# A gated mix of a Fourier layer and 32-head attention on one core: named PSUM banks and a freed value bank in the 52 short sections

## The chip, the cores and the metric

The kernel runs on one core of a Trainium2 chip. The metric is the device time of one execution in microseconds (us); lower is better. A core has a matrix engine (TensorE, PE in the profile; its weight loads are PEld), a vector engine (VectorE, DVE), an activation engine (ScalarE, ACT), GpSimd (POOL) and SyncE (SP), which here issues most of the transfers. Each engine runs its own instructions in their order and waits on semaphores for the others. PE writes its results to PSUM, eight banks of 128 partitions x 512 fp32 numbers; here ACT and DVE read them out.

## The reference

```python
x = A_x                                            # 1 x 2048 x 512
g = sigmoid((x * gate_w).sum(-1, keepdims=True))
a = Ws_re @ (x @ Wd_re.T) - Ws_im @ (x @ Wd_im.T)  # Fourier mixing: 512 wide, then 2048 long
q, k, v = split(B_x @ wqkv)                        # B_x is x; 32 heads of 16
p = softmax(q @ k.T * 16 ** -0.5)                  # per head, 2048 x 2048
b = (p @ v, heads put side by side) @ wo
out = g * a + (1 - g) * b
```

All in fp32. The inputs of the products are split into a high and a low part, and three products stand for one.

## The kernel before, in words

After the projections of q, k and v the kernel is one long stream. Attention is done per pair of heads `p` (16 pairs) and per half of the queries. The work on it comes in three kinds:

- **a**, a product for a maximum (`a_tile`, L291): 128 queries x 512 keys into a bank; DVE then takes the row maximum (L293).
- **s**, a score (`scores`, L795): 128 keys x 512 queries into a bank; ACT then writes its exponential to a tile `pt` in SBUF (L796). Four scores fill one `pt`, called a unit `u`.
- **values** (`pv`, L843): for one unit, four products of `pt` with `vt`, added up in the bank `acc`. `vt` has a column of ones beside each head's values, so that the sum of the exponentials comes out as a further row.

a and s have 64 rows or fewer, half of PE's array, and run beside a **d** on the other half: a product of the other layer (L469), whose 128 rows are cut into two halves. The first half of a d chain is done in one segment, the second half in the next. So PE's work goes in *slots*: two products side by side, mostly a d and one of a and s, sometimes (a "double") two of a and s without a d.

`segment` walks a pattern, written out by hand, one word for each slot. A small letter is the a or s beside the d; a second, capital letter makes the slot a double, whose second product is from the other half's stream; `|` is the four value products of one unit. A digit behind a letter names the bank. Each segment has eight a and eight s on average and two units of values. There are three kinds of segments:

| pattern | segments | slots in them | d chains | order and place of values |
|---|---|---|---|---|
| `THIN` | 13 pairs | 14 and 14 | `real`, 12 products | before the last 4 slots, and at the end |
| `FULL` | 96 pairs | 16 and 16 | `dft`, 48 products over three pairs | both at the end |
| `NINE` | 13 pairs | 12 and 13 | `proj`, 9 products | before the last 3 or 4 slots, and at the end |

Of the eight banks one is `d`, and seven are numbered. In `FULL` every a and s names its bank, 0 to 6: bank 6 is that of `acc`, and it can take an a and a score, because at a FULL segment's end the values are closed (`close`): ACT copies `acc` to an SBUF tile `part` (L822; the first one goes to `oe`, L816), POOL adds that to a running total `oe` (L823), and the next segment's values begin a fresh sum. In `THIN` and `NINE` the letters have no digits. There a `Ring` gives the bank used longest ago: scores among 0, 1, 2, maxima among 3, 4, 5. Bank 6 keeps `acc` alone, and it is copied only when a pair of heads is done with one half of the queries (every 16 units, eight segments) and once at the end of `THIN`.

A d chain ends in one ACT copy of bank `d`: `y` in `THIN` (L485), `few` in `NINE` (L665, followed by a POOL add, L666). The next chain's first d waits for it. Between the two halves of a chain, the second half's first d is made to wait (`add_manual_dep`) for the reader of one product that stood behind the first half's last d: the exponential of the *last* such s, or the maximum of the first such a where there is no s.

Of the kernel before, what the change touches and what calls it, by code (L numbers as in the profile page):

```python
# [20 lines left out]
NP = H // 2  # L21
KT = D // P
NT = S // P
# [8 lines left out]
def mix_kernel(ctx: ExitStack, tc: tile.TileContext, xa_t, xa, wqkv, w_hid, w_seq, wo, gate_w, out):  # L32
# [227 lines left out]
    vt = main.tile([P, NT, NP, 33], F32, name="vt")  # L260
# [24 lines left out]
    def a_tile(i, h, ps=None, bank=None):  # L285
        p, j = divmod(i, 64)
        qt, kb = divmod(j, 4)
        if ps is None:
            ps = psA.tile([P, 512], F32, "a", bank)
        r = slice(64 * h, 64 * h + (64 if p else 48))  # L290
        nc.tensor.matmul(ps, qs[p % 2][r, qt * P:(qt + 1) * P], ks[p % 2][r, kb * 512:(kb + 1) * 512],  # L291
                         start=True, stop=True)
        user = nc.vector.tensor_reduce(mx[p % 2][:, h, qt, kb:kb + 1], ps, AX.X, ALU.max)  # L293
        hf = j // 32
        a_left[p, hf] = a_left.get((p, hf), 64) - 1
        if not a_left[p, hf]:
            deferred.extend((partial(m_parts, p, hf), partial(m_rows, p, hf)))
        return user
# [483 lines left out]
    def scores(u, qb, h, bank=(psS, "s"), number=None):  # L782
        p, r = divmod(u, 32)
        hf, kt = divmod(r, 16)
        q0 = hf * 1024 + qb * 512
        if u >= UNITS - 16:

            blk, kt = divmod(kt, 8)
            q0, kt = 1024 + blk * 512, 2 * kt + qb
        if u not in pts:  # L790
            pts[u] = work.tile([P, 4, 512], F32, name="pt", bufs=4)
        pool, name = bank
        ps = pool.tile([P, 512], F32, name=name) if number is None else pool.tile([P, 512], F32, name, number)
        rr = slice(64 * h, 64 * h + (64 if p else 50))
        nc.tensor.matmul(ps, ks[p % 2][rr, kt * P:(kt + 1) * P], qs[p % 2][rr, q0:q0 + 512], start=True, stop=True)  # L795
        return nc.scalar.activation(pts[u][:, 2 * qb + h], ps, AF.Exp, bias=0.0, scale=DH ** -0.5)  # L796

    def pv_last(u):
        blk, k2 = divmod(u - UNITS + 16, 8)
        pt = pts.pop(u)  # L800
        for j in range(4):
            x, h = divmod(j, 2)
            nc.tensor.matmul(acc[32 * j:32 * j + 17], vt[:, 2 * k2 + x, NP - 1, 16 * h:16 * h + 17], pt[:, j],  # L803
                             start=k2 == 0, stop=k2 == 7)
        if blk == 0 and k2 == 7:
            last_pairs.append(LastPair(0, [(psS, "s"), (psA, "a")]))
            last_pairs[0].copy(1)
# [3 lines left out]
    def evacuate(p, hf, done):  # L811

        nonlocal total
        if total is None:
            total = work.tile([P, 512], F32, name="oe", bufs=2)
            nc.scalar.copy(total, acc)  # L816
        else:
            if not part:
                two = work.tile([P, 2, 512], F32, name="part", tag="w15")
                part.extend(two[:, i] for i in range(2))  # L820
            part.reverse()
            nc.scalar.copy(part[0], acc)  # L822
            nc.gpsimd.tensor_tensor(total, total, part[0], ALU.add)  # L823
        if done:
            for qb in range(2):
                nc.sync.dma_start(o_d[hf][p, :, qb * 512:(qb + 1) * 512], total[64 * qb:64 * qb + 64])
            total = None

    def pv(u, close=False):
        nonlocal acc  # L830
        if u >= UNITS - 16:
            return pv_last(u)
        p, r = divmod(u, 32)
        hf, kt = divmod(r, 16)
        pt = pts.pop(u)
        begin, done, width = acc is None or kt == 0, kt == NT - 1, 17
        if acc is None:
            acc = psO.tile([P, 512], F32, "acc")
            width = 32
        v = vt[:, kt].rearrange("p n d -> p (n d)")[:, 33 * p:]  # L840
        for j in range(4):
            h = j % 2
            i = nc.tensor.matmul(acc[32 * j:32 * j + width], v[:, 16 * h:16 * h + width], pt[:, j],  # L843
                                 start=begin, stop=done or close)
        if done or close:
            evacuate(p, hf, done)
            if close:
                acc = None
        return i
# [35 lines left out]
    for hf in range(2):  # L885
        for ct in range(4):
            n = 3 if hf and ct == 3 else 4
# [31 lines left out]

    FULL = "a5 s4 a2 s0 a3 s6 a5 s4 s1 s0 s2 a6 a3 a4 s5 a1 | |"  # L920
    START = "sA s aS - - a s - - a s - - a", "s a s a s a s a s a s a +s +a"
    THIN = "s a s a s a s a s a | s a aS sA |", "aS a s s a s a s a s | s a a sA |"
    NINE = "a s a s a s a s a | sS sA aA |", "aS s a s a s s a aS | s a sA sA |"

    def stream(h):

        return (
            iter([(u, qb, h) for u in range(UNITS) for qb in range(2)]),
            iter([(i, h) for i in range(lead, NP * 64)]),
        )  # L930

    thin = 1 + 4 * (NT - 3)
    streams = [stream(h) for h in range(2)]

    users, valued, exponentials = [], 0, []

    def score(kind, h, number=None):
        x = next(streams[h][kind == "a"], None)
        if x:
            users.append((kind, a_tile(*x, bank=number) if kind == "a" else scores(*x, number=number)))  # L940
            if kind == "s":
                exponentials.append(users[-1][1])

    def values(close=False):
        nonlocal valued
        i = pv(valued, close)
        valued += 1
        return i

    def segment(pattern, half, ds, stop):  # L950


        nonlocal users, full_now
        full_now = pattern == FULL
        before, users = users, []
        ds, turned = iter(ds), False
        for n, slot in enumerate(pattern.split()):
            number = None
            if slot[1:].isdigit():
                slot, number = slot[0], int(slot[1])  # L960
            if slot == "|":
                end = n == len(pattern.split()) - 1
                i = values(end and (pattern == FULL or valued == thin))
                if end and pattern == FULL:

                    tc.add_manual_dep(i.ins, exponentials[-2].ins.name,
                                      mybir.DependencyInfo(mybir.DependencyClass.Sync, mybir.DependencyReason.DATA))
                while between:
                    between.pop(0)()
                if deferred and pattern in NINE and not turned and "|" in pattern.split()[n + 1:]:  # L970
                    deferred.pop(0)()
                    turned = True
                continue
            if not n and number is not None:

                score(slot, 1 - half, number)
            if len(slot) == 1:
                x = next(ds, None)
                if x:

                    before = before if x[0].begun else None
                    i = issue(x, half, stop)
                    users = []
                    if before:
                        tc.add_manual_dep(
                            i.ins, dict(before).get("s", before[0][1]).ins.name,
                            mybir.DependencyInfo(mybir.DependencyClass.Sync, mybir.DependencyReason.DATA))
                        before = None
            if slot != "-" and (n or number is None):
                score(slot[-1] if slot[0] == "+" else slot[0], 1 - half, number)  # L990
            if len(slot) == 2 and slot[0] != "+":
                score(slot[1].lower(), half)

        while full_now and deferred:
            deferred.pop(0)()
        if deferred and not (pattern in NINE and (turned or len(deferred) == 1)):
            deferred.pop(0)()

    def pairs():

        for i in range(NT - 3):
            yield THIN, take(hid, 12)
        for i in range(2 * NT * 3):
            yield FULL, take(seq, 16)
        for gen, n in ((proj(1, (0, 1, 2), one), 8), (first, 5)):
            for i in range(n):
                yield NINE, take(gen, 9)

    first = proj(0, (0, 1, 2), one * 5 + two[:1] + one, range(7))
# [8 lines left out]
    pump(hid, 12)  # L1018
    segment(START[1], 1, ds, True)
    values()  # L1020
    values()
    for patterns, ds in pairs():
        for half in range(2):
            run_plan(valued)
            pattern = FULL if patterns is FULL else patterns[half]
# [69 lines left out]
```

## Time and profile before

| | |
|---|---|
| median of 3 runs | 1670.02 us (1669.85 to 1670.27) |
| the profiled execution | 1669.9 us, its span 1668.1 us |
| granted PE clock | 0.999 |
| ACT exponentials, L796 | 2006, 1022.8 us |
| DVE maxima, L293 | 2026, 1257.0 us |
| value products, L843 | 3968 records, 496 units of 8 |
| ACT copies of acc, L822 and L816 | 169 and 31 |

The first row is what a changed kernel is compared with. The rows of the profile come from one execution; it is within 0.1 us of the median. The span is the time from the first to the last instruction on the core, and the 1.8 us by which the execution is longer lie around it. Each fp32 value product stands in the trace as two records, so one unit is eight records. In the timeline and in the chain of waits the columns are: start in us from the span's start, length in us, what it is; `x8` says that eight instructions in a row were merged.

### The profile page before, as it was taken

What the parts mean: (1) busy time and instruction counts of PE and PEld (TensorE: products, weight loads), DVE (VectorE), ACT (ScalarE), POOL (GpSimd) and SP (SyncE); (2) the same over time, 40 slices, a digit from 0 to 9 for tenths busy, and PEclk for the clock granted to TensorE, in tenths of its full rate; (3) what the DMA queues carried; (4) which work ended last, traced back from release to release, by engine and by line L of the source; (5) the groups of instructions that cost most, each with busy time, mean ns of one, the idle gap of its engine ahead of it and who ended that gap; (6) DMA issues with size and microseconds to landing.
All of it is one profiled execution on the core that took longest, in us unless ns stands there. A gap on an engine that the chain in (4) does not pass through costs nothing.

```text
span 1668.1 us, 34619 instructions
## 1 busy us (share of the span) xinstructions
PE 1660.8 (100%) x13040; PEld 1012.7 (61%) x13040; DVE 1378.0 (83%) x2361; ACT 1242.1 (74%) x2423; POOL 660.1 (40%) x688
## 2 busy tenths in 40 slices
PE   9999999999999999999999999999999999999998
PEld 7888755556566655665566556665666566544543
DVE  5439888888888888888888888888888888888954
ACT  5212377788878888888788878887888888888886
POOL 0202112234444456544444466554445556421110
PEclk9999999999999999999999999999999999999999
DMA  9963610414151342414147444314142535462114
GB/s 292 350 158 121 178 20 2 70 33 84 39 97 47 69 110 82 96 46 78 46 91 253 85 120 100 84 56 87 53 84 59 110 103 124 147 179 37 40 30 139
DMA packets 82690, 166.70 MB, mean 100 GB/s; under 512 B 19665, under 2 KB 20159, under 8 KB 78511
## 3 DMA queue, kind: packets, MB, share of 16 engines
q1 hardware_dynamic: 78282, 163.53, 38.8%
q8 instruction: 103, 1.69, 0.5%
q0 software_dynamic: 3808, 0.30, 0.2%
q14 instruction: 65, 0.52, 0.1%
q10 hardware_dynamic: 432, 0.66, 0.1%
HBM read 109.14 MB, written 54.65 MB: 98 GB/s over the span
## 4 chain that ended last, share of the span: by engine, by line
PE 99%; DMA 0%; DVE 0%; DVEq 0%; issue 0%
PE acc L843 28%; PE d L469 25%; PE a L291 18%; PE s L795 15%; PE s L383 3%; PE s L415 1%; PE d L383 1%; PE acc L803 1%; PE a L108 1%; PE a L107 1%; PE s L108 1%; PE s L107 1%; PE a L106 1%; PE s L106 1%; PE s L469 1%; PE a L469 1%
## 5 line engine op out<-in xcount | busy, mean ns | idle before, releaser
L293 DVE TENSOR_REDUCE mx<-a 128x1 f32<-128x512 f32 x2026 | 1257.0, 683 | 178.0 <-PE a L291 153.7
L796 ACT ACTIVATE pt<-s 128x512 f32<-128x512 f32 x2006 | 1022.8, 623 | 67.6 <-PE s L795 57.7
L291 PE MATMUL a<-ks,qs 64*128 64x512 f32 (+1 forms) x2026 | 725.0, 404 | 0.0
L795 PE MATMUL s<-qs,ks 64*128 64x512 f32 (+1 forms) x2006 | 690.0, 400 | 0.0
L469 PE MATMUL d<-xab,ch 64*128 64x512 f32 x2016 | 644.8, 394 | 0.0
L291 PEld LDWEIGHTS a<-ks,qs 64*128 64x128 f32 (+1 forms) x2026 | 365.8, 184 | 215.1 <-issue 123.7
L843 PE MATMUL acc<-pt,vt 128*17 128x512 f32 (+1 forms) x3968 | 486.5, 598 | 0.0
L823 POOL TENSOR_TENSOR oe<-oe,part 128x512 f32<-128x512 f32 x169 | 218.5, 1293 | 502.4 <-ACT part L822 497.3
L795 PEld LDWEIGHTS s<-qs,ks 64*128 64x128 f32 (+1 forms) x2006 | 364.9, 184 | 59.9 <-issue 16.8
L469 PE MATMUL d<-xab,cl 64*128 64x512 f32 x1008 | 397.9, 395 | 0.0
L469 PEld LDWEIGHTS d<-xab,ch 64*128 64x128 f32 x2016 | 366.7, 184 | 28.0
L822 ACT COPY part<-acc 128x512 f32<-128x512 f32 x169 | 99.1, 587 | 182.0 <-PE acc L843 181.4
L843 PEld LDWEIGHTS acc<-pt,vt 128*17 128x17 f32 (+1 forms) x3968 | 91.5, 101 | 213.7 <-issue 151.6
L469 PEld LDWEIGHTS d<-xab,cl 64*128 64x128 f32 x1008 | 185.6, 184 | 13.5
L454 POOL TENSOR_TENSOR cl<-craw,ch 128x512 fp32r<-128x512 f32 x126 | 162.1, 1287 | 10.1
L469 PE MATMUL d<-wre,xab 64*128 64x512 f32 x336 | 90.6, 402 | 0.0
L453 POOL CAST ch<-craw 128x512 fp32r<-128x512 f32 x126 | 76.9, 610 | 16.6 <-PE s L795 10.6
L469 PEld LDWEIGHTS d<-wre,xab 64*128 64x128 f32 x336 | 58.8, 184 | 38.6 <-issue 23.3
L323 POOL DMA_DIRECT2D qs<-mt x119 | 67.0, 568 | 26.9 <-PE a L291 9.5
L469 PE MATMUL d<-wo_hl,o_hl 64*128 64x512 f32 (+1 forms) x246 | 68.2, 409 | 0.0
L469 PEld LDWEIGHTS d<-wo_hl,o_hl 64*128 64x128 f32 (+1 forms) x246 | 42.3, 184 | 29.8 <-issue 12.2
L487 POOL CAST xab<-y 128x512 fp32r<-128x512 f32 x16 | 9.7, 609 | 127.3 <-ACT y L485 99.2
(172 smaller groups left out, 1038.0 us busy)
## 6 DMA issues: line engine op xcount, KB each, us to landing
craw<-w_seq SPq DMA_DIRECT2D x128, 256.0 KB
qk<-hl SPq DMA_DIRECT2D x32, 512.0 KB
qs<-qk SPq DMA_DIRECT2D x96, 128.0 KB
ks<-qk SPq DMA_DIRECT2D x96, 128.0 KB
b<-hl SPq DMA_DIRECT2D x16, 512.0 KB
xab<-b SPq DMA_DIRECT2D x16, 512.0 KB
o<-oe SPq DMA_DIRECT2D x62, 128.0 KB
oh<-nh SPq DMA_DIRECT2D x12, 512.0 KB
```

What stands on the lines that cost most here:

```text
L291: nc.tensor.matmul(ps, qs[p % 2][r, qt * P:(qt + 1) * P], ks[p % 2][r, kb * 512:(kb + 1) * 512], start=True, stop=True)
L293: user = nc.vector.tensor_reduce(mx[p % 2][:, h, qt, kb:kb + 1], ps, AX.X, ALU.max)
L323: (nc.gpsimd if own else nc.sync).dma_start(rows.rearrange("v (q b c) -> v b q c", q=8, b=4)[:, b], mt[hf][32 * b + h:32 * b + 32:2])
L383: i = nc.tensor.matmul(ps, st[r], mv[r], start=not half and not j, stop=half == 1 and j == 11)
L453: nc.gpsimd.tensor_copy(h1, raw)
L454: nc.gpsimd.tensor_tensor(l1, raw, h1.bitcast(F32), ALU.subtract)
L469: i = nc.tensor.matmul(self.ps, st[r], mv[r], start=not self.begun, stop=stop)
L795: nc.tensor.matmul(ps, ks[p % 2][rr, kt * P:(kt + 1) * P], qs[p % 2][rr, q0:q0 + 512], start=True, stop=True)
L796: return nc.scalar.activation(pts[u][:, 2 * qb + h], ps, AF.Exp, bias=0.0, scale=DH ** -0.5)
L822: nc.scalar.copy(part[0], acc)
L823: nc.gpsimd.tensor_tensor(total, total, part[0], ALU.add)
L843: i = nc.tensor.matmul(acc[32 * j:32 * j + width], v[:, 16 * h:16 * h + width], pt[:, j], start=begin, stop=done or close)
```

## The change

- Every a and s of `THIN` and `NINE` names its bank, among 0 to 6; a double's second letter has its own digit. The numbers of slots, of d, a and s, and of value units in a segment are the same as before; their order is another one. The values in the middle now stand before the last 3 or 4 slots in `THIN` and before the last 2 in `NINE`.
- The values are closed at the end of every segment (`values(end)`), and after the two units ahead of `THIN`. So `acc` is copied by ACT and added by POOL once a segment, as in `FULL`. In the changed program this is 48 ACT copies and 48 POOL adds more. Bank 6 takes one score in each of these segments.
- Between the halves of a chain the second half's first d waits for the exponential of the *first* s behind the first half's last d (`dict(reversed(before))`).
- The first values of a segment load weights 32 columns wide where they were 17, as in `FULL`; `vt` is sliced over the tile border so that this fits for the last pair of heads.

```diff
-        v = vt[:, kt].rearrange("p n d -> p (n d)")[:, 33 * p:]
+        v = vt.rearrange("p t n d -> p (t n d)")[:, 33 * (NP * kt + p):]
...
-    THIN = "s a s a s a s a s a | s a aS sA |", "aS a s s a s a s a s | s a a sA |"
-    NINE = "a s a s a s a s a | sS sA aA |", "aS s a s a s s a aS | s a sA sA |"
+    THIN = ("a1 s0 s5 a2 a4 s6 s3 s0 a1 a5 s2 | a3 a4S1 s5A0 |",
+            "a2 s4 a1 s3 a0 s6 a5 s2 a4 s3S1 | a5A0 s3 a4 s2 |")
+    NINE = ("a3 s0 s5 a4 a1 s6 s3 a0 a2 s5A4 | s5S1 a3A0 |",
+            "a2S4 a5 s1 a3 s0 s6 a4 a1 s5S2 s0 a3 | s5A4 s1A2 |")
...
-    thin = 1 + 4 * (NT - 3)
...
-            number = None
-            if slot[1:].isdigit():
-                slot, number = slot[0], int(slot[1])
+            number, other = None, None
+            if slot[1:2].isdigit():
+                number, other = int(slot[1]), int(slot[3]) if slot[2:] else None
+                slot = slot[::2]
+            first = not n and pattern == FULL
...
-                i = values(end and (pattern == FULL or valued == thin))
+                i = values(end)
...
-            if not n and number is not None:
+            if first:
                 score(slot, 1 - half, number)
...
-                            i.ins, dict(before).get("s", before[0][1]).ins.name,
+                            i.ins, dict(reversed(before)).get("s", before[0][1]).ins.name,
...
-            if slot != "-" and (n or number is None):
+            if slot != "-" and not first:
                 score(slot[-1] if slot[0] == "+" else slot[0], 1 - half, number)
             if len(slot) == 2 and slot[0] != "+":
-                score(slot[1].lower(), half)
+                score(slot[1].lower(), half, other)
...
     segment(START[1], 1, ds, True)
     values()
-    values()
+    values(True)
```

## The prediction

> **What bounds the kernel now.** I read the page first, then the chain of waits for the starts of the value blocks, then the busy times by stretch.
>
> ```profile
> span 1668.1 us, 34619 instructions
> ```
>
> The chain of waits is a list of PE's own work, so I take PE's pace in the three kinds of sections from it: the starts of the value blocks (`x8` is one unit, `x16` two in a row).
>
> ```profile
> 217.48 0.98 PE acc L843 x8
> ...
> 255.53 0.98 PE acc L843 x8
> 257.65 0.98 PE acc L843 x8
> 261.26 0.98 PE acc L843 x8
> ...
> 354.73 0.98 PE acc L843 x8
> ...
> 365.46 1.85 PE acc L843 x16
> ...
> 1459.32 1.85 PE acc L843 x16
> ...
> 1471.12 0.98 PE acc L843 x8
> ...
> 1595.38 0.98 PE acc L843 x8
> 1597.26 0.99 PE acc L843 x8
> ...
> 1602.99 0.98 PE acc L843 x8
> ```
>
> 365.46 to 1459.32 is 190 FULL segments, 5.757 us each: 16 slots and two blocks, of which the second adds 1.85 - 0.98 = 0.87. So 16 slots and one block take 4.887. From 255.53 to 257.65, in THIN, 4 slots and one block take 2.12. The difference gives 2.767 / 12 = 0.2306 us for a slot, and 2.12 less four slots gives 1.20 for a block with its way in and out. That is PE's undisturbed pace. (3 slots and a block, 1595.38 to 1597.26, take 1.88; by these figures 1.89.)
>
> At this pace a THIN pair (28 slots, 4 blocks) takes 6.46 + 4.79 = 11.25 us, and a NINE pair (25 slots, 4 blocks) 5.76 + 4.79 = 10.55. They do take (354.73 - 217.48) / 12 = 11.44 and (1602.99 - 1471.12) / 12 = 10.99. The losses are 0.19 and 0.44 a pair, over 13 pairs each 2.5 and 5.7: **8.2 us in all** is what any order of slots with the same count can win. The loss sits in the long stretches between blocks: 257.65 to 261.26 is 3.61 for 10 slots, where 3.51 would do.
>
> Who is late there is not an engine that is full:
>
> ```profile
> 217.41:354.66 137.25, 137.25 (x1058) 72.37 (x1057) 119.42 (x199) 106.57 (x209) 33.91 (x45) 1.00 0.18 30
> 365.51:1459.37 1093.86, 1093.86 (x9124) 662.01 (x9126) 960.17 (x1647) 890.82 (x1742) 553.01 (x561) 1.00 0.38 90
> 1471.06:1602.92 131.86, 131.86 (x983) 65.46 (x981) 117.48 (x197) 107.19 (x209) 26.41 (x34) 1.00 0.23 51
> ```
>
> These are the busy times by stretch (PE, PEld, DVE, ACT, POOL) for 12 THIN pairs, the FULL part and 12 NINE pairs. A NINE pair has 9.79 us of DVE and 8.93 of ACT in 10.99. PE loses its time to banks that are not yet read out when their turn comes, three for scores and three for maxima, and to the handover of a d chain:
>
> ```profile
> PEld d L469 <- ACT pt L796: 1.9, 12, 0.2
> ```
>
> (the waits between 1461 and 1603: in total, times, longest).
>
> **What a late bank costs.** Two moments of a NINE segment in which a score waits for its bank:
>
> ```profile
> 1488.47 0.61 ACT L822 COPY part<-acc 128x512 f32<-128x512 f32 x1
> 1488.94 0.65 ACT L796 ACTIVATE pt<-s 128x512 f32<-128x512 f32 x1
> ```
>
> ```profile
> 1489.64 0.18 PEld L795 LDWEIGHTS s<-qs,ks 64*128 64x128 f32 x1
> 1489.70 0.18 PEld L469 LDWEIGHTS d<-wo_hl,o_hl 64*128 64x128 f32 x1
> 1490.13 0.18 PEld L795 LDWEIGHTS s<-qs,ks 64*128 64x128 f32 x1 [0.25 <-ACT pt L796]
> ```
>
> ```profile
> 1489.92 0.39 PE L469 MATMUL d<-wo_hl,o_hl 64*128 64x512 f32 x1
> ...
> 1490.47 0.39 PE L291 MATMUL a<-ks,qs 64*128 64x512 f32 x1
> ```
>
> The copy occupies ACT for 0.47 until the exponential behind it starts; this exponential ends at 1489.59, and the weights of the score that takes its bank go at 1489.64, 0.05 later. The wait stands at the weight load, which is otherwise done beside the slot ahead. The d's load at 1489.70 shows when the next score's was due; it went at 1490.13, 0.43 late. The next slot should have started one slot after 1489.92, at 1490.15, and started at 1490.47, 0.32 late. So 0.11 of lateness costs nothing, and the rest costs its full length.
>
> **The change part by part.**
>
> *Slots, blocks and products* are the same in number, so PE's floor stays at 11.25 and 10.55. The 32-wide weights cost nothing: FULL, whose first block has them, is where the pace was taken from.
>
> *The copies.* 48 more on ACT at 0.47 are 23 us, two in a pair: 106.57 / 12 + 0.94 = 9.82 of 11.25 in THIN and 8.93 + 0.94 = 9.87 of 10.55 in NINE. There is room, but a copy stands ahead of a segment's first exponentials and pushes them. Behind the copy are queued the segment's scores, and PE waits for those. From FULL, where every segment does it:
>
> ```profile
> 603.58 0.50 PE L291 MATMUL a<-ks,qs 64*128 64x512 f32 x1
> 603.58 0.72 PE L469 MATMUL d<-xab,ch 64*128 64x512 f32 x2
> 603.92 0.39 PE L795 MATMUL s<-qs,ks 64*128 64x512 f32 x1
> ```
>
> ```profile
> 603.80 0.59 ACT L822 COPY part<-acc 128x512 f32<-128x512 f32 x1 [1.17 <-PE acc L843]
> 604.35 4.03 ACT L796 ACTIVATE pt<-s 128x512 f32<-128x512 f32 x8
> ```
>
> Count from a segment's first slot. The second starts at 0.34, then one each 0.23: slot n at 0.34 + 0.23 (n - 2). The copy starts at 0.22, the next exponential at 0.69 or, for a score in slot 2, 0.43 after its product (603.92 to 604.35), at 0.77. Eight take 4.03: with 0.60 for one, the spacing is 0.49.
>
> ```profile
> 604.12 5.04 DVE L293 TENSOR_REDUCE mx<-a 128x1 f32<-128x512 f32 x8 [0.28 <-PE a L291]
> ```
>
> A maximum starts 0.54 after the product of the first slot, and eight take 5.04, 0.63 each.
>
> *THIN's banks.* A bank must be released by the start of the slot ahead plus 0.11. First segment: s0 of slot 2 ends at 1.37, released 1.42; s0 of slot 8 is due at 1.49. s5 of slot 3 is released at 1.91; a5 in slot 10 is due at 1.95. Second segment: s3 of slot 4 is the second exponential, released at 1.91, for slot 10: the same. Bank 6 of slot 6 is the third, released at 2.40, and the values begin ten slots and the way in later, at 2.5. The handover waits for S1, which ends a block ahead. So I expect no stall: 2.5 us won. If one bank a pair is late by 0.1 beyond the allowance, 1.3 go.
>
> *NINE's banks, first segment.* s0 of slot 2 for a0 in slot 8, s5 of slot 3 for slot 10, bank 6 for the values: the same times as above, in time. a4 of slot 4 (0.80) is the second maximum: it starts at 1.34 at the latest, is released at 2.02, and A4 in slot 10 is due at 1.95, inside the allowance. The handover, the 1.9 us of the waits, goes: its d now waits for s5 of slot 10, long done.
>
> *NINE's banks, second segment.* It begins `a2S4 a5 s1 ... a4 a1`. S4 stands in slot 1, so its exponential starts right behind the copy, at 0.69; that of s1 at 1.18, ending at 1.78, released at 1.83. a1 in slot 8 takes the same bank, and its weights are due at 1.49. It is 0.34 late, less 0.11: **a stall of 0.23 us in each pair**, 3.0 us over 13. The slots behind it move along, and with them their own demands. So of NINE's 5.7 us, 2.7 are won. What is late next is a3 in slot 11, behind the third maximum (0.54 + 3 x 0.63, released 2.48, due 2.18 + 0.23): 0.07, inside the allowance.
>
> The Trainium skill ("ScalarE: Activation LUTs", section "What ACT_TABLE_LOAD costs") gives an activation with immediate operands as 186 ns + 0.833 ns an element, with 93 ns of overlap between neighbours. For 512 elements that would be, as an estimate from that page, 0.61 long and 0.52 apart. The rows agree with the length (0.60) and not with the spacing (0.49, and 0.47 behind a copy); by the page s1 would be released about 0.08 later, and the sum would lose 1.0 us more. I go by the rows.
>
> *POOL.* 48 more adds. The trace shows one in a NINE section:
>
> ```profile
> 1489.16 1.29 POOL L823 TENSOR_TENSOR oe<-oe,part 128x512 f32<-128x512 f32 x1 [5.06 <-ACT part L822]
> ```
>
> Two in a pair are 2.6 us on a POOL that has 26.41 / 12 = 2.2 busy of 10.99 in NINE and 2.8 in THIN. `part` has two halves, so a copy waits only for the add of two segments earlier, about 5 us of cover. If that cover is gone, ACT waits, and all scores with it.
>
> *The last total.* The sums of the last pair's first half now end in a copy and an add where they ended in a copy: 1.3 us later into the last output product. Its input was ready in time:
>
> ```profile
> 1639.40 1.23 DVE L630 TENSOR_TENSOR o_l<-o_raw,o_l 128x1024 fp32r<-128x1024 f32 x1
> ```
>
> ```profile
> 1643.78 0.96 PE L469 MATMUL a<-wo_hl,o_l 128*128 128x512 f32 x3
> ```
>
> Ready at 1640.63, used at 1643.78: 3.1 us of cover. Nothing.
>
> **The sum.** 2.5 in THIN and 2.7 in NINE, 5.2 us off a profiled execution of 1669.9 us, 1.8 longer than its span; it stands 0.1 below the median. From the median: 1670.0 - 5.2, in round figures **1665.0 us**.
>
> **The rivals.**
>
> *No stall at all.* If the copy starts sooner than 0.22, or a1 has more allowance than one case showed, all 8.2 us go: 1661.8. For: the way FULL holds its pace with the same copies. Against: s1's margin is negative by 0.23 where FULL's similar reuse (s4, slots 2 and 8) is positive by 0.07.
>
> *The waits only change places.* Scores and maxima now share banks, so DVE's and ACT's delays reach each other. If the new reuses are as late as the old ones, only the handover goes: 1.9 us in NINE and, for THIN's second segment (3.61 against 3.51), 13 x 0.10 = 1.3, against the new stall of 3.0. Then 1669.8, which is no change. For: DVE has 9.79 us of work in 10.55, little air. Against: the walk finds the reuses nearest to each other, in slots 8 and 10, due after their release or within the allowance, all but one.
>
> *The copy lands on the path in every segment.* If a segment's first exponentials decide its pace, each of 52 copies costs 0.47 less the allowance of 0.11, 18.7 us, and less the 8.2 won: 1670.0 + 10.5 = 1680.5. It decides where the second exponential of a segment ends later than 1.55 and its bank is asked for again by slot 8, or where POOL frees a half of `part` late. For: one segment of four, NINE's second, is so laid out. Against: the three others ask for that bank in slot 10 or later, and FULL does the same 192 times at 5.757.
>
> **How the numbers follow.** The forecast as walked, 1664 to 1666.5: 0.55. No stall, about 1662: 0.13. Waits that change places, within 0.2% (3.3 us, about what a measurement of this kernel can tell from no change): 0.17. Copies on the path, wholly or in part: 0.15. The range takes in the first three, 1661.5 to 1669.8. Faster by over 0.2% is the first two, 0.68; within it 0.17; slower 0.15.
>
> **What would show it.** In the profile after, value blocks of THIN 3.74 and 1.89, then 3.51 and 2.12 apart; of NINE 3.51, 1.66, then 3.97 (3.74 with the stall) and 1.66. In NINE's second segment the weights of the eighth slot's a wait for ACT. FULL stays at 5.757. I am wrong if THIN's pairs stay above 11.35, if the wait of that a is missing, or if another score or maximum waits in every pair.

## The result, and the profile after

The changed kernel takes 1666.43 us (median of 13 runs, 1665.53 to 1667.16) against 1670.02 before (13 runs, 1669.50 to 1670.37): a ratio of 0.9979, 95% interval 0.9971 to 0.9986, 3.6 us faster. The forecast was 1665.0. The profiled execution takes 1666.87 us. Here are the first line of the page of after, and its busy times by stretch (PE, PEld, DVE, ACT, POOL) for 12 THIN pairs and 12 NINE pairs:

```profile
span 1665.0 us, 34810 instructions
```

```profile
218.02:353.51 135.49, 135.49 (x1058) 69.12 (x1057) 120.38 (x199) 118.38 (x229) 60.55 (x66) 1.00 0.19 31
...
1469.60:1598.79 129.19, 129.19 (x982) 62.57 (x980) 118.31 (x196) 117.37 (x229) 52.25 (x54) 1.00 0.24 51
```

They answer to those of 137.25 and 131.86 before. A THIN pair now takes 135.49 / 12 = 11.29 us (forecast 11.25), a NINE pair 129.19 / 12 = 10.77 (forecast 10.78). ACT has 9.87 and 9.78 us of work in them, where 9.82 and 9.87 were expected. The value blocks in the chain of waits of after:

```profile
252.22 0.98 PE acc L843 x8
255.98 0.99 PE acc L843 x8
257.86 0.99 PE acc L843 x8
...
358.57 1.85 PE acc L843 x16
...
1458.04 1.85 PE acc L843 x16
1462.40 1.00 PE acc L843 x8
1464.06 0.98 PE acc L843 x8
1468.01 1.00 PE acc L843 x8
1469.67 0.98 PE acc L843 x8
```

NINE: 1458.92 (where the second block of the merged 16 starts) to 1462.40 is 3.48, then 1.66, 3.95 and 1.66, against a forecast of 3.51, 1.66, 3.97 and 1.66. (In the prediction's "3.97 (3.74 with the stall)" the words in brackets should read "without the stall": 11 slots and a block are 2.54 + 1.20 = 3.74.) The block has the stall: 3.95 is 0.21 above 3.74. It is as long in 12 of the 13 pairs; in the last it takes 3.78. FULL: 1458.04 - 358.57 over 191 segments is 5.756, as before.

The whole span can be cut at five value blocks: the first, the second (where THIN begins), the 54th (FULL), the 438th (NINE) and the 490th (the end section). The lengths, in us:

| kernel | to the first block | THIN | FULL | NINE | 490th to 512th block |
|---|---|---|---|---|---|
| before | 205.14 | 148.65 | 1105.47 | 142.79 | 53.67 |
| after | 205.85 | 146.79 | 1105.34 | 139.94 | 54.76 |
| difference | +0.7 | -1.86 | -0.1 | -2.85 | +1.1 |

The first column is before anything that was changed; over all kernels of this study it lies between 204.8 and 206.2, so it is not a part of the change. What was won in THIN and NINE is 4.7; 1.1 is lost again in the end section; the difference, 3.6, is that of the medians (that of the two spans, 3.1, has the 0.7 of the start in it). Two questions follow: is the stall of NINE what the prediction said it was, and where do the 1.1 us at the end come from?

The stall first. NINE's second segment in the timeline of after; slot 1 starts at 1508.12.

```profile
1508.31 0.59 ACT L822 COPY part<-acc 128x512 f32<-128x512 f32 x1 [0.22 <-PE acc L843]
1508.79 3.05 ACT L796 ACTIVATE pt<-s 128x512 f32<-128x512 f32 x6
```

```profile
1509.61 0.18 PEld L469 LDWEIGHTS d<-wo_hl,o_hl 64*128 64x128 f32 x1
1509.94 0.18 PEld L291 LDWEIGHTS a<-ks,qs 64*128 64x128 f32 x1
...
1510.10 0.19 PEld L469 LDWEIGHTS d<-wo_hl,o_hl 64*128 64x128 f32 x1
1510.43 0.18 PEld L795 LDWEIGHTS s<-qs,ks 64*128 64x128 f32 x1
```

```profile
1509.84 0.39 PE L469 MATMUL d<-wo_hl,o_hl 64*128 64x512 f32 x1
...
1510.06 0.60 PE L795 MATMUL s<-qs,ks 64*128 64x512 f32 x2
1510.33 0.39 PE L469 MATMUL d<-wo_hl,o_hl 64*128 64x512 f32 x1
...
1510.56 0.39 PE L469 MATMUL d<-wo_hl,o_hl 64*128 64x512 f32 x1
1510.76 0.38 PE L291 MATMUL a<-ks,qs 64*128 64x512 f32 x1
```

The copy starts 0.19 into the segment, S4's exponential at 0.67, s1's one spacing of 0.49 later, at 1.16, and it ends some 0.60 behind that, at 1508.12 + 1.76 = 1509.88. The weights of the a in slot 8, which takes that bank, go at 1509.94. Its d had them at 1509.61: 0.33 late. Slot 9 is a double without a d, so the d's of 1509.84 and 1510.33 are two slots apart, 0.49 where 0.46 is due: the d's lose 0.03. The loss is in the products beside them. The a of slot 11 starts at 1510.76, 0.20 behind its d; by the pace it was due at 1508.12 + 0.34 + 9 x 0.23 = 1510.53, so it is 0.23 late, as forecast.

A second bank is late in the same stretch, and the prediction did not list it. The s0 of slot 10 takes the bank of slot 5's s0, the third exponential, which ends at 1508.79 + 2 x 0.49 + 0.60 = 1510.37. Its weights go at 1510.43, 0.33 behind those of its d. It adds nothing here, because the a of slot 8 has already put these products back: the second score of slot 9 (the end of the merged line, 1510.66, less 0.39) starts at 1510.27, 0.20 late, and the two behind it keep that distance.

Now the end. DVE and PE in the timeline of after, near the last output product:

```profile
1636.85 0.70 DVE L629 CAST o_l<-o_raw 128x1024 fp32r<-128x1024 f32 x1 [3.95 <-POOL o_raw L643]
1637.58 1.22 DVE L630 TENSOR_TENSOR o_l<-o_raw,o_l 128x1024 fp32r<-128x1024 f32 x1
1638.72 0.74 DVE L668 SCALAR_TENSOR_TENSOR yp<-d,omg,yp 128x512 f32<-128x512 f32 x1
1639.38 0.20 DVE L734 RECIPROCAL rc<-s 128x8 f32<-128x8 f32 x1
1639.62 0.35 DVE L736 TENSOR_TENSOR on<-s,rc 128x64 f32<-128x64 f32 x2
```

```profile
1636.02 1.00 PE L732 MATMUL s<-pairsum,oe 128*128 128x64 f32 x8
...
1640.12 0.47 PE L795 MATMUL s<-qs,ks 64*128 64x512 f32 x1 [0.59 <-DVE on L736]
```

The bracket is idle time of the engine and what ended it. PE waits in a stretch where it did not wait before (and once more, 0.17 us for L668, at 1625.71). It waits for a bank that L736 reads out. L734 and L736 are short, and the product that they read (L732) ended at 1637.02. But they stand behind L629, L630 and L668 in DVE's order, and L629 had waited 3.95 us for POOL's product (L643), that for a transfer (`o_raw<-r`), and that in the end for the sums. Before, DVE's order was the same, and L629 waited less:

```profile
1638.67 0.69 DVE L629 CAST o_l<-o_raw 128x1024 fp32r<-128x1024 f32 x1 [2.11 <-POOL o_raw L643]
```

Counted from the 490th value block (1602.92 before, 1598.79 after) L629 starts at 35.75 before and at 38.06 after, 2.3 later; before, PE waited for no bank here. In the chain of waits of after this is the path:

```profile
1616.81 1.30 POOL oe L823
...
1618.69 2.37 DMA o<-oe
...
1621.73 2.12 DMA rc<-o
...
1627.80 1.94 DMA r<-rc
...
1630.41 3.87 DMA o_raw<-r
1634.44 2.39 POOL o_raw L643
```

### The profile page after: what moved, and what is told of

It reads as the page before. It is cut to its first block, busy times and chain, and to the rows that moved or that the text cites. A ratio compares the mean times of both kernels' runs of the same rounds, so it can differ in the third digit from the quotient of the medians.

```text
span 1665.0 us, 34810 instructions
## 1 busy us (share of the span) xinstructions
PE 1655.8 (99%) x13040; PEld 1008.9 (61%) x13040; DVE 1380.5 (83%) x2361; ACT 1266.4 (76%) x2469; POOL 720.2 (43%) x734
## 4 chain that ended last, share of the span: by engine, by line
PE 98%; DMA 1%; DVE 0%; issue 0%; POOL 0%; ACT 0%; SPq 0%; DVEq 0%; POOLq 0%; ACTq 0%
PE acc L843 28%; PE d L469 24%; PE a L291 18%; PE s L795 16%; PE s L383 3%; PE s L415 1%; PE d L383 1%; PE a L108 1%; PE a L106 1%; PE s L108 1%; PE s L106 1%; PE a L107 1%; PE s L107 1%; PE a L469 1%; PE s L469 0%; DMA raw<-xa_t 0%
## 5 line engine op out<-in xcount | busy, mean ns | idle before, releaser
L795 PE MATMUL s<-qs,ks 64*128 64x512 f32 (+1 forms) x2006 | 664.2, 395 | 0.8 <-DVE on L736 0.6
L823 POOL TENSOR_TENSOR oe<-oe,part 128x512 f32<-128x512 f32 x215 | 278.4, 1295 | 597.4 <-ACT part L822 594.9
L291 PEld LDWEIGHTS a<-ks,qs 64*128 64x128 f32 (+1 forms) x2026 | 361.2, 184 | 213.7 <-issue 118.2
L822 ACT COPY part<-acc 128x512 f32<-128x512 f32 x215 | 126.3, 588 | 187.5 <-PE acc L843 186.5
L102 ACT CAST hl<-s 128x512 fp32r<-128x512 f32 x28 | 16.2, 588 | 58.9 <-PE s L383 31.3
```

## The experiments

**The handover's wait alone.** The kernel before with one word of the change.

```diff
-    i.ins, dict(before).get("s", before[0][1]).ins.name,
+    i.ins, dict(reversed(before)).get("s", before[0][1]).ins.name,
```

> The kernel before with one edit: the second half's first d waits for the first s behind the first half's last d, not the last; patterns, rings and closing as before. Theory A (the bank rings are what is late in the long stretches): the 1.9 us of handover waits in the short sections go, but the scores behind them then wait as much longer for their banks; the value blocks after the doubles at a segment's start stay within 0.05 us of 3.60 in NINE and 3.61 in THIN, and the time is 1669.5, within 0.6 us of before. Rival (the prediction's pricing of the handover): the waits were on the path, 1.9 us in NINE and 13 x 0.10 in THIN go, 1666.8.

1669.69 us against 1669.73 on the same chip, ratio 0.9999 (0.9990 to 1.0008). The wait of 1.9 us that the prediction showed is gone from the list of waits. The 12 NINE pairs take 131.81 where they took 131.86. In place of the handover the scores wait longer, in a row that stood at 1.3 us, 6 times, before:

```profile
PEld s L795 <- ACT pt L796: 3.7, 14, 0.3
```

So those 1.9 us were in front of work that was late anyway. These waits of the weight loader were no loss of PE. The list of waits of after has a far larger row of the same name, and the pairs are shorter:

```profile
PEld d L469 <- ACT pt L796: 10.2, 12, 0.9
```

Twelve times 0.85: this is the loader's idle time while a value block runs, put down to the last release before it.

**THIN alone and NINE alone.** In each, the changed kernel with the other group's old patterns, whose values are not closed within it. The handover's new wait stays in both groups.

```diff
 # THIN alone
+    NINE = "a s a s a s a s a | sS sA aA |", "aS s a s a s s a aS | s a sA sA |"
...
-                i = values(end)
+                i = values(end and pattern not in NINE)
 # NINE alone
+    THIN = "s a s a s a s a s a | s a aS sA |", "aS a s s a s a s a s | s a a sA |"
...
+    thin = 1 + 4 * (NT - 3)
...
-                i = values(end)
+                i = values(end and (pattern not in THIN or valued == thin))
...
-    values(True)
+    values()
```

> The changed kernel with NINE's old patterns, rings and open sums: the change in THIN alone (the handover edit holds in both groups). Theory A (each group pays for itself, and what was lost again was lost at the end through the later last total, which this kernel does not have): THIN pairs at 11.29 us for 11.44, 1.9 us won, no later value block at the end: 1668.1. Rival (the end's 1.1 us in the changed kernel is luck of its transfers, or comes from the earlier groups): 1 us slower or faster at the end without a later total, 1667 to 1669, and the stretches after the last NINE segment other than before.

> The changed kernel with THIN's old patterns, rings and open sums: the change in NINE alone. Theory A: NINE pairs at 10.77 us for 10.99, 2.8 us won, and 1.1 us given back at the end, where the last total now passes through ACT and POOL: 1670.0 - 2.8 + 1.1 = 1668.3. Rival (the end's loss is not from the total): 1667.2, with the end as before.

| kernel | median | ratio | THIN | NINE | 490th to 512th block |
|---|---|---|---|---|---|
| THIN alone | 1668.14 | 0.9989 (0.9981 to 0.9998) | 146.79 | 142.72 | 53.67 |
| NINE alone | 1668.38 | 0.9991 (0.9983 to 1.0000) | 148.62 | 139.95 | 55.16 |

Each part wins in its own section just what it wins in the whole, 1.86 and 2.84. The loss at the end comes with NINE alone. With THIN alone the sums of the last pair's first half still end in one copy to `oe`, and nothing is lost there.

**The late total alone.** The kernel before; only the last pair's first half ends in a copy and a POOL add.

```diff
-                nc.scalar.copy(total, acc)
+                if p == NP - 1 and hf == 0 and done:
+                    nc.gpsimd.memset(part[1], 0.0)
+                    nc.scalar.copy(part[0], acc)
+                    nc.gpsimd.tensor_tensor(total, part[0], part[1], ALU.add)
+                else:
+                    nc.scalar.copy(total, acc)
```

> The kernel before with one edit: the sums of the last pair's first half go through an ACT copy into part and a POOL add of zeros (1.29 us) into the total, instead of an ACT copy into the total; nothing else of the change. Theory A (the end has no cover for this: DVE takes its instructions in order, and two that free a score bank stand behind two that wait for transfers of these sums): 0.8 to 1.2 us slower, 1671.1, with a PE wait for the DVE multiply of line 736 (its line in the kernel before) of over 0.4 us and a later block after it. Rival (the prediction: 3.1 us of cover before the product that uses the sums): 1670.0.

The end section takes 55.02, 1.35 more than before; THIN (148.47) and NINE (142.76) stay. The time is 1670.39 against 1669.73, ratio 1.0004 (0.9995 to 1.0013): too small a step to be told by the time alone, but the profile has it in the same place as after, with PE waiting 1.1 us for L736. Behind this product L629 starts at 1641.00, after 4.44 us of idle DVE:

```profile
1638.59 2.38 POOL L643 TENSOR_TENSOR o_raw<-o_raw 128x1024 f32<-128x1024 f32 x1 [16.75 <-DMA o_raw<-r]
```

**The end's order.** The changed kernel, with the row of sums asked for two units later, the reciprocals behind it too, and the split of `o_raw` (L629, L630) two units later. The work is the same; DVE's order is another.

```diff
-            at(last + (12 if ct < 3 else 4), inverse, hf, ct, n)
+            at(last + (12 if ct < 3 else 4 + 2 * (hf == 0)), inverse, hf, ct, n)
-    for step, u in ((0, 498), ("sums", 500), (1, 504), (2, 506)):
+    for step, u in ((0, 498), ("sums", 502), (1, 504), (2, 508)):
```

> The changed kernel with the planned times of three steps at the end moved: the inverse of the last sums and the load behind it from unit 500 to 502, the split of the last product's input from 506 to 508, so that on DVE they stand behind the two instructions that free score banks. Nothing is taken out. Theory A (the later total costs through DVE's order alone): the end, from the last NINE block to the last pair's last block, goes from 54.8 us back to 53.7 or less, 1665.3. Rival (the later total delays the product itself, so it is only moved): 54.8 or more, 1666.4 or slower.

```profile
1636.66 0.36 DVE L736 TENSOR_TENSOR on<-s,rc 128x64 f32<-128x64 f32 x2
1637.47 0.69 DVE L629 CAST o_l<-o_raw 128x1024 fp32r<-128x1024 f32 x1 [0.45 <-POOL o_raw L643]
```

L736 now stands ahead of L629. Both waits of PE are gone, the end section takes 53.87 in place of 54.76, and the time is 1665.46 against 1670.33, ratio 0.9972 (0.9961 to 0.9982). POOL's product is not earlier, it is later (1635.06 for 1634.43, in a profile that is 0.4 ahead at the 490th block): what cost time was the place in DVE's order, not the transfers by themselves. The Trainium skill ("Perfetto Trace Analysis", section "Tensor Engine Instruction (MATMUL, LD_WEIGHTS)") calls the queues of ACT, DVE and GpSimd strict first-in first-out and PE's reorder limited; for DVE the rows of after agree: L734 starts at 1639.38, behind L629, though its product had ended at 1637.02.

The size of the loss differs from profile to profile. Seven kernels have the late total and DVE's old order at the end (the changed one, NINE alone, the late total alone, and four below); their end sections take 54.28 to 55.16. The three with the old total (before, the handover alone, THIN alone) take 53.67 to 53.69. So the loss lies between 0.6 and 1.5 us, and 1.1 is what one profile shows. The two kernels with the other order, 53.87 here and 54.15 below, lie under all seven.

**Which reuse stalls in NINE.** Theory: between copy and first values, 13 products lie on seven banks in the second segment, so whichever digits are used, the bank that is still missing comes free about 0.2 us late. Rival: it is that one pair, s1 and a1, and another choice of numbers is free of the stall. The changed kernel, the banks of one a and some s exchanged, the order of a and s alike:

```diff
-            "a2S4 a5 s1 a3 s0 s6 a4 a1 s5S2 s0 a3 | s5A4 s1A2 |")
+            "a2S4 a5 s1 a3 s0 s6 a2 a4 s1S5 s0 a3 | s1A4 s5A2 |")
```

> The changed kernel with other digits in NINE's second segment alone: a2S4 a5 s1 a3 s0 s6 a2 a4 s1S5 s0 a3 | s1A4 s5A2. The eighth slot no longer takes the bank of s1 but that of S4, released 0.5 us sooner. Theory B (thirteen products on seven banks before the values: whichever digits, ACT releases the bank that is still missing 0.2 us late): the stall moves to a score in the ninth or tenth slot, the long block stays at 3.95 within 0.1, the time at 1666.4. Rival C (the pairing of s1 and a1 is the stall, as the prediction put it): the block at 3.74, 13 x 0.21 = 2.7 us won, 1663.7.

1666.05 us (0.9976, 0.9966 to 0.9986), NINE 140.05. The chain of waits of this kernel has the block as long as it was, 1510.65 - 1506.70 = 3.95:

```profile
1506.70 0.98 PE acc L843 x8
1510.65 1.00 PE acc L843 x8
```

```profile
1507.61 0.18 PEld L291 LDWEIGHTS a<-ks,qs 64*128 64x128 f32 x1 [0.85 <-DVE mx L293]
...
1509.12 0.18 PEld L291 LDWEIGHTS a<-ks,qs 64*128 64x128 f32 x1
1509.43 0.24 PEld L795 LDWEIGHTS s<-qs,ks 64*128 64x128 f32 x2
1509.59 0.19 PEld L469 LDWEIGHTS d<-wo_hl,o_hl 64*128 64x128 f32 x1
1509.92 0.18 PEld L795 LDWEIGHTS s<-qs,ks 64*128 64x128 f32 x1
```

Slot 1 begins at 1507.61. The weights of slot 8's a go 1.51 later, in time (due at 1.49). The first of slot 9's two scores, which takes the bank of the second exponential, has its weights at 1509.43, 1.82 behind the start: 0.10 late, inside the allowance, and its product starts at 1509.56, on the pace. The late one is now the s0 of slot 10. Its weights go at 1509.92, 0.33 behind those of its d, 2.31 behind the start and 0.05 behind the end of the third exponential (1509.87). In after the same score's weights went at 1510.43 - 1508.12 = 2.31. So there are two late banks in after's stretch; the second one alone makes the whole stall, and to free only the first is worth nothing. The rival falls.

**One double less ahead of the values.** By the same theory 11 products on seven banks leave room. One double of NINE's second segment is moved behind the values, so that no bank of the third or a later exponential is asked for ahead of them; the first segment's last two doubles trade letters with it.

```diff
-    NINE = ("a3 s0 s5 a4 a1 s6 s3 a0 a2 s5A4 | s5S1 a3A0 |",
-            "a2S4 a5 s1 a3 s0 s6 a4 a1 s5S2 s0 a3 | s5A4 s1A2 |")
+    NINE = ("a3 s0 s5 a4 a1 s6 s3 a0 a2 s5A4 | s5A1 s3A0 |",
+            "a2S4 a5 s1 a3 s6 s0 s2 a4 a1 s5 | s0A3 s2A4 s5A1 |")
```

> The changed kernel with another distribution in NINE: first segment a3 s0 s5 a4 a1 s6 s3 a0 a2 s5A4 | s5A1 s3A0, second a2S4 a5 s1 a3 s6 s0 s2 a4 a1 s5 | s0A3 s2A4 s5A1. Same counts over a pair; one double fewer before the values of the second segment and one more behind them, and the first segment gives its other stream no score but three maxima. Theory B (two doubles in the long stretch are one more than seven banks carry): no stall, NINE pairs at 10.55 to 10.60 for 10.77, 2.4 us won, 1664.0. Rival D (the copies' time on ACT or the eight maxima a segment bound NINE at its pace): pairs stay at 10.7 or above and the waits go elsewhere, 1665.8 or slower.

1669.07 us (0.9992, 0.9983 to 1.0001): NINE takes 142.16, nearly what it took before. The expected time was missed, and the theory held for the long stretch: the blocks are 3.50, 1.66, 3.49 and 2.28. The long stretch has lost its stall (3.95 to 3.49). The loss sits in the new stretch of three doubles, 2.28 (2.26 to 2.29 in most pairs) where 3 slots and a block take 1.89. ACT and PEld there:

```profile
1512.31 0.74 ACT L665 ACTIVATE few<-d,omg 128x512 f32<-128x512 f32 x1
```

```profile
1513.59 0.18 PEld L795 LDWEIGHTS s<-qs,ks 64*128 64x128 f32 x1 [0.55 <-ACT pt L796]
```

The s5 of slot 10 is the last product ahead of the values, so its exponential comes behind `few` (0.57 until the next instruction starts), the copy of the d chain that ends in the same slot. It ends at about 1513.5, and the s5 of the last double waits for its bank until 1513.59, 0.55 after the loader was free. I had put no price on that place in ACT's queue.

**The same, and the last two single slots exchanged.** If that is the cause, it is enough to let the a and not the s stand beside the last d. This differs from the kernel above in two words only:

```diff
-            "a2S4 a5 s1 a3 s6 s0 s2 a4 a1 s5 | s0A3 s2A4 s5A1 |")
+            "a2S4 a5 s1 a3 s6 s0 s2 a4 s5 a1 | s0A3 s2A4 s5A1 |")
```

> The changed kernel, with NINE's second segment as ten slots, values, and three doubles, so that 11 products instead of 13 lie on the seven banks between the copy and the first double; behind the values one more slot stands, and its long stretch ends in an a, so that the last single score's exponential can stand ahead of the copy `few` on ACT. Theory (two doubles too many ahead of the values cause the wait of a1; ACT's queue behind `few` caused the wait of the other layout): blocks 3.50, 1.66, 3.51 to 3.57, 1.89 to 1.95, a NINE pair 10.56 to 10.68, the NINE part 2.0 to 3.0 us shorter than the changed kernel's 139.94 (137 to 138), the time 1663.5 to 1664.8. Rival (NINE is held by ACT, or by eight maxima of DVE in a segment, whatever the order): the wait shows up at another slot, the pair stays at 10.75 or above and the time at 1666 or above.

1664.41 us (1664.11 to 1665.07) against 1670.22 on the same chip, ratio 0.9966 (0.9954 to 0.9979). The blocks and the 12 pairs:

```profile
1462.03 1.00 PE acc L843 x8
1463.69 0.98 PE acc L843 x8
1467.21 1.00 PE acc L843 x8
1469.11 0.98 PE acc L843 x8
```

```profile
1469.04:1596.06 127.02, 127.02 (x982) 62.49 (x981) 117.59 (x196) 115.60 (x229) 52.17 (x54) 1.00 0.24 52
```

1.66, 3.52 and 1.90 are seen here (3.50, 1.66, 3.51 and 1.89 in most pairs, as expected); a pair takes 10.585, 0.03 above the undisturbed 10.55. ACT has 115.60 / 12 = 9.63 us and DVE 9.80 of work in it: neither holds it. The rival (ACT or DVE holds NINE whatever the order) falls. That the count of 13 or 11 products decides by itself is argued from the moments at which the banks come free; two orders of each count were run.

**Both orders together.** This NINE and the end's order.

```diff
+    NINE = ("a3 s0 s5 a4 a1 s6 s3 a0 a2 s5A4 | s5A1 s3A0 |",
+            "a2S4 a5 s1 a3 s6 s0 s2 a4 s5 a1 | s0A3 s2A4 s5A1 |")
...
+            at(last + (12 if ct < 3 else 4 + 2 * (hf == 0)), inverse, hf, ct, n)
...
+    for step, u in ((0, 498), ("sums", 502), (1, 504), (2, 508)):
```

> The run before it together with the tail order (the row of sums and the reciprocals of the last half two and four slots later). If the two act apart, the gains add up: the tail 0.9 us shorter, value blocks at the end 3.2 and 4.7 apart, 1662.5 to 1664.0. If the shorter NINE brings the reciprocals forward into another maximum's way, the tail stays at 54.5 or above, and the time is that of the run before it.

1663.42 us (1663.02 to 1663.90), ratio 0.9959 (0.9946 to 0.9973): no run of it is as slow as the fastest of the run before, on the same chip. It is 6.8 us below the kernel before, the changed kernel 3.6. The end section takes 54.15 where it took 54.84. Not all of NINE's gain stays: the stretch behind NINE's last block takes 6.03 where it took 5.78 in after and 5.60 before. In the chain of waits it is ACT's queue that runs through that border, from 1592.33 on (the lines left out are its exponentials); the 0.25 was not taken apart further:

```profile
1595.86 0.57 ACT few L665
...
1597.69 0.70 ACT part L822
```

**The copies without the new orders.** The kernel before with the values closed in every segment; the orders and banks of the short sections stay.

```diff
-        v = vt[:, kt].rearrange("p n d -> p (n d)")[:, 33 * p:]
+        v = vt.rearrange("p t n d -> p (t n d)")[:, 33 * (NP * kt + p):]
...
-                i = values(end and (pattern == FULL or valued == thin))
+                i = values(end)
...
-    values()
+    values(True)
```

> The kernel before with the sums closed, copied and added once a segment in the short sections, as in the changed kernel, but with the old patterns and rings (bank 6 stays with the sums) and the old handover. Theory A (a copy pushes the first exponentials, and with three score banks these are at once needed): 0.11 us more in each second segment of NINE and about as much in THIN's, so NINE 144.0 and THIN 150.0 for 142.8 and 148.65, and about 1 us at the end: 1673.4. Rival (there is room on ACT, so the copies are free as long as their bank is not shared): only the end is later, 1670.7.

1674.08 us against 1670.33, ratio 1.0022 (1.0013 to 1.0031): slower by 3.7. THIN takes 150.03, NINE 144.27, the end section 55.13: 1.4, 1.5 and 1.5 more than before. The blocks tell where: the first segment of a pair keeps its pace (3.55 and 2.12 in THIN, 3.32 and 1.89 in NINE), the second has one stretch that takes 3.72 in most pairs where it took 3.61. Over 13 pairs that is 1.1 of the 1.4 and of the 1.5.

## Why the prediction was right, and where it was not

- *PE's pace and the floor*: right. FULL holds 5.756, and the best NINE comes within 0.03 us of the 10.55 that was worked out.
- *The copies*: right that ACT has room for them (9.87 and 9.78 us a pair) and that they cost nothing in the new order. This rests on the new banks and orders: in the old ones they cost 2.9 us in THIN and NINE, beside what the old waits cost already. The rival "the copy lands on the path in every segment" priced that at 18.7; the mechanism is there, at a sixth of the size. The trace has 46 more copies and 46 more adds (215 for 169), where 48 were named; two in a pair is right. No run has the new orders without bank 6, so what the freed bank is worth by itself stays open.
- *THIN's banks*: right that no bank stalls in every pair, over-sized by 0.6: won are 1.86, forecast 2.5. The term took all of the 0.19 a pair as winnable. The pairs now take 11.20 us in the later part (3.71, 1.89, 3.48, 2.12), less than the 11.25, and 11.30 in the first pair of heads (3.76, 1.88, 3.53, 2.13); in two of the 13 pairs one stretch takes 0.2 more (3.92 to 3.96). In both, the a of slot 1 starts 0.24 behind its d (320.92 for 320.68 in the second of them); what holds it was not tried.
- *NINE's banks, second segment*: right in place and size, and short by one cause. a1 in slot 8 waits for the exponential behind S4's, 0.33 late where 0.34 was forecast, and 2.85 us were won where 2.7 were. But the s0 of slot 10 waits in every pair too, which was named as a sign of being wrong. By the prediction's own figures its bank is released at 0.69 + 2 x 0.49 + 0.60 + 0.05 = 2.32 and due at 1.95, a stall of 0.26 beyond the allowance; the walk passed over it. That the size held is luck: the two waits cover each other, and without a1's the stall is as long (3.95). The rival "no stall at all" falls. The other NINE order shows what that would have been worth: 2.35 more (137.59).
- *What is late next*: wrong as named, since s0 in slot 10 comes before a3 in slot 11. Right that nothing is lost behind a1: the whole block is 0.21 above 3.74, no more than the one stall.
- *The handover*: wrong where it was priced. The 1.9 us of the waits were to go as a gain in the rival "the waits only change places". Alone it moves the time by -0.04 us and the 12 pairs by -0.05. The sum was not built on it. The rival as a whole falls too: each group alone wins 1.9 and 2.8 us in its section.
- *POOL*: right. No copy waits for its add: of the idle time ahead of the copies, 186.5 of 187.5 us end with PE's values. On the page of after:

```profile
L822 ACT COPY part<-acc 128x512 f32<-128x512 f32 x215 | 126.3, 588 | 187.5 <-PE acc L843 186.5
```

- *The last total*: the step that failed. "3.1 us of cover. Nothing" compared the time at which `o_l` is ready with the time at which its product uses it, and that cover did hold (in after it is ready at 1637.58 + 1.22 = 1638.80, and its product comes behind the score of 1640.12, at 1640.78). The cost is beside it: DVE takes its instructions in order, L629 comes later, and behind it in DVE's order stand L668, L734 and L736, whose reads set the banks of scores free. It was 1.1 us in the profile of after; the late total alone costs 1.35, and with the other order of DVE the section is 0.9 shorter. The other 0.2 lie in the first stretch behind NINE (5.78 where it was 5.60), which no step had.
- *The sum*: 5.2 forecast; 4.7 won in THIN and NINE, 1.1 lost at the end, 3.6 measured.

## What to carry to other kernels

When a value comes later, it is not enough to ask whether its last user still has it in time: list what is queued behind its *first* reader on that engine, and who waits for those. In a rotation of banks write down every reuse between the copy and the next pause, when its bank comes free and when it is due, and not only those that look nearest: behind one late bank a second can stand that is as late. Give the late places (behind the copy, behind a chain's read-out) to products that nobody follows closely; two exchanged words were worth 4.7 us here (1669.07 to 1664.41, on two chips whose kernel before takes 1670.33 and 1670.22). Read a wait of the weight loader as a loss only where the next product's start is late too.

## What the runs showed of the hardware that was not expected

- Late by 1.3 us at the sums became late by 2.3 at the product behind four transfers (L643 at 1638.59 with the late total, 1636.26 before). The four legs of after took 2.37, 2.12, 1.94 and 3.87 us. The issue times show where the added 1.0 us lie: `r<-rc` goes 1.3 later (1631.34 for 1630.04), `o_raw<-r` 1.8 later (1633.87 for 1632.11). So they lie in the last two legs; why these took longer was not tried.
- The time to the first value block, the same code in all kernels, was between 204.8 and 206.2 us in the profiled executions. A difference of 1 us between two profiles says nothing before it is cut by stretch.
